# One hundred and twenty-eight products on a buffer of zeros, in sixteen groups, behind the clock-keeping products of an attention and gated-MLP kernel

## The chip, the cores and the metric

The kernel runs on one core of one Trainium2 chip. The metric is the device time of one execution in microseconds, as the median of several runs. The host only lays the arrays out.

## The reference

Attention inside chunks of 64 positions (8 batches, 8 heads, 576 positions, 64 channels), followed by an MLP with a spatial gate (model width 512, inner width 1024):

```python
# q, k, v: (8, 8, 576, 64), cut into 9 chunks of 64 positions
scores = matmul(q_c, k_c.T) / 8
attn = softmax(scores)                       # inside a chunk
x = matmul(attn, v_c)                        # laid out as (8, 576, 512)
h = gelu_tanh(x @ w_in)                      # (8, 576, 1024)
u, v = h[..., :512], h[..., 512:]
v_n = (v - mean(v)) / sqrt(var(v) + 1e-6) * g_ln
v_s = einsum('ts,bsd->btd', w_sg, v_n) + b_sg
out = x + (u * v_s) @ w_out
```

All inputs are float32. The three weight matrices reach the chip as 64-bit words and `w_sg` as float32.

## The kernel before

**The work.** The 8 batches of 576 positions make 36 attention tiles of 128 rows (two chunks each). For each batch there are four or five `v` units (`v_unit`, 128 tokens by 512 columns), four `u` units, four `s` units and four `o` units. Nearly every large product is taken three times, on a high and a low part of each operand in `F32R`, so that float32 accuracy is kept: a `v` unit is 12 products of 512 columns (L452), a `u` unit 24 of 288 columns (L489), an `s` unit 28 of 288 (L509), an `o` unit 24 of 288 (L532).

**The order.** `START` is a table of steps written out by hand for the first two batches; behind it a loop goes through the units of the other six, with attention steps in slots between them. The tile framework then schedules what the steps record, engine by engine, so the order on an engine is not that of the table. Its first steps are

```python
L0 A0 L1 A1 L2 L3 A4 W0 S0 W1 D8 w0 S1 W2 T0 w1 S2 O0 T1 W3 w2 S3 O1 T2 M0 w3 S4 O2 T3 v00 ...
```

`L` loads a weight block and `A` an attention tile, both on the SP queue. `W` (`pair_begin`) splits a block of `w_in` on VectorE and ScalarE (L130 to L133, L162, L166, L174); `w` (`pair_end`) makes its low part on TensorE (L178: a float32 product, two bf16 products and an `F32R` product, all of 512 columns) and takes it out on ScalarE (L179), and then loads a further block over the staging tile. `S` is a tile's scores (L314, 16 products of 64 by 64) and softmax (L333 to L358), `T` its transposition (L366, L368), `O` its output (L398) and the split of that (`keep`, L94, L97, L428, L438). A softmax is done head by head on ScalarE for tiles 0, 2 and 4 (L344) and in whole on VectorE and ScalarE for the others (L346, L349).

**The place of the change.** `D8` calls `keep_clock(8)` (L573 to L577): eight float32 products of the 128 by 128 identity with itself into a PSUM tile that nobody reads. They stand behind the scores of tile 0 (`S0`) and ahead of `w0` on TensorE. `ident` is the float32 view of `ident_r`, which ScalarE casts to `F32R` (L103) from a tile that GpSimd fills (`make_identity`, in masks.py). In the staging, `wsg_106`, `wsg_111`, `wout_115` and `wout_117` are the tiles of the blocks of `W0` to `W3`; `low_86` and `low_87` are two scaled bf16 identities. The tile `v` of the first `v` unit is taken from pool `mp` under the tag `v`, of which there is one buffer.

Of the kernel before, what the change touches and what calls it, by code (L numbers as in the profile page):

```python
# [10 lines left out]
F32 = mybir.dt.float32  # L11
F32R = mybir.dt.float32r
# [3 lines left out]
BF16 = mybir.dt.bfloat16  # L16
# [6 lines left out]
P = 128  # L23
DM = 512
DF = 1024
DH = DF // 2
# [54 lines left out]
def block_attention_gated_mlp(ctx: ExitStack, tc: tile.TileContext, qkv, w_in, w_out, w_sg, g_ln, b_sg, out):  # L81
    nc = tc.nc
# [3 lines left out]
    mp = ctx.enter_context(tc.tile_pool(name="mp", bufs=1))  # L86
# [15 lines left out]
    ident_r = const.tile([P, P], F32R, name="ident")  # L102
# [470 lines left out]
    def keep_clock(n):  # L573

        spare = ps_m.tile([P, 2, 512], F32, name="pm")
        for _ in range(n):
            nc.tensor.matmul(spare[:, 0, :P], ident, ident, start=True, stop=True)  # L577

    steps["D"] = keep_clock
    steps["G"], steps["g"] = lambda k: load_w_sg(), split_w_sg  # L580
# [56 lines left out]
```

## Time and profile before

| what | value |
|---|---|
| timed runs | 507.87 and 510.36 us, median 509.12 us |
| profiled execution, first to last instruction (span) | 505.7 us |
| TensorE (PE) matmul busy | 493.4 us, 98% of the span, 5238 instructions |
| VectorE (DVE) busy | 339.2 us, 67% |
| ScalarE (ACT) busy | 274.2 us, 54% |
| GpSimd (POOL) busy | 70.0 us, 14% |
| share of the chain that ended last, by engine | PE 83%, DVE 7%, ACT 5%, DMA 3%, POOL 1% |
| read from HBM, written | 36.34 MB, 9.44 MB |

The page gives the profiled execution as its span alone; the median of the two timed runs is 3.4 us above that span. Rows give line, engine, operation, output and inputs with their shape, a count, and the busy time and mean duration of one. PE is a matmul, PEld the load of its stationary matrix; a float32 product is recorded as two matmuls, an `F32R` or bf16 product as one. Matmuls are pipelined, so that the duration of one (0.40 us for 512 columns in L452) is longer than the time from its start to the next one's start. What a product costs in a stream is therefore read from starts and counts, not from durations.

### The profile page before, as it was taken

Reading aid. Unit: us, or ns where it says so; the run is one execution under the profiler, and the core shown is the slowest. Engines: PE = TensorE matmul, PEld = TensorE weight load, DVE = VectorE, ACT = ScalarE, POOL = GpSimd, SP = SyncE. Lnnn points to the kernel's source line nnn. Section 1 sums busy time; section 2 is a strip of 40 time slices with the busy share of each in tenths; the row PEclk is TensorE's granted clock in tenths of the full one; section 3 lists DMA queues with packets and bytes.
Section 4 is the critical chain, followed back from the end, with each engine's and each line's share of the span. In section 5 each row is a group of like instructions: output and inputs, shape, how many; then the busy total and the mean of one; then the engine's idle time right before and its main releaser. Section 6 shows DMA issues by size and latency. Waiting matters only on the chain.

```text
span 505.7 us, 12377 instructions
## 1 busy us (share of the span) xinstructions
PE 493.4 (98%) x5238; PEld 457.1 (90%) x5244; DVE 339.2 (67%) x707; ACT 274.2 (54%) x509; POOL 70.0 (14%) x72
## 2 busy tenths in 40 slices
PE   5999999999999999999999999999999999999996
PEld 4667899799998899989999899989999899999996
DVE  7998779987856947585563966676565776536141
ACT  5898667843346674355552774355643766334210
POOL 0112100210201401022100311022100131002000
PEclk9999999999999999999999999999999999999999
DMA  8958010237166113341324204160415200010002
GB/s 336 331 144 224 3 43 2 85 97 197 48 201 199 55 36 93 101 119 46 82 73 148 64 1 128 47 174 2 126 37 160 87 1 3 23 73 0 1 1 93
DMA packets 49595, 46.58 MB, mean 92 GB/s; under 512 B 35202, under 2 KB 39554, under 8 KB 49540
## 3 DMA queue, kind: packets, MB, share of 16 engines
q1 hardware_dynamic: 49540, 45.80, 29.9%
q8 instruction: 41, 0.67, 0.6%
q14 instruction: 14, 0.11, 0.1%
HBM read 36.34 MB, written 9.44 MB: 91 GB/s over the span
## 4 chain that ended last, share of the span: by engine, by line
PE 83%; DVE 7%; ACT 5%; DMA 3%; POOL 1%; issue 1%; DVEq 0%; SPq 0%; ACTq 0%; POOLq 0%
PE pm L509 20%; PE pm L532 19%; PE pm L489 18%; PE pm L452 17%; PE banks L322 3%; PE pm L410 3%; DMA qkv_t<-qkv 2%; PE pm L178 2%; DMA st<-w_out 1%; ACT pt L344 1%; PE pm L314 1%; POOL sm L461 1%; DVE v L470 1%; DVE gl L97 1%; PE pm L577 1%
## 5 line engine op out<-in xcount | busy, mean ns | idle before, releaser
L509 PE MATMUL pm<-wsg,v 128*128 128x288 f32 x768 | 107.9, 296 | 0.0
L509 PEld LDWEIGHTS pm<-wsg,v 128*128 128x128 f32 x768 | 103.9, 189 | 0.3
L532 PE MATMUL pm<-gh,wout 128*128 128x288 f32 x512 | 92.3, 297 | 0.0
L532 PEld LDWEIGHTS pm<-gh,wout 128*128 128x128 f32 x512 | 76.1, 189 | 0.5
L461 POOL TENSOR_TENSOR sm<-sm,neg_half 128x1 f32<-128x1 f32 x36 | 36.6, 1017 | 164.9 <-DVE sm L460 161.5
L358 POOL TENSOR_TENSOR pt<-pt,den 128x512 f32<-128x512 f32 x27 | 29.7, 1113 | 202.2 <-DVE den L357 128.3
L94 ACT CAST gh<-gt 128x576 fp32r<-128x576 f32 x32 | 21.5, 673 | 63.5 <-DVE gt L513 63.5
L532 PE MATMUL pm<-gl,wout 128*128 128x288 f32 x256 | 55.4, 296 | 0.0
L489 PE MATMUL pm<-xh,win_l 128*128 128x288 f32 x256 | 55.4, 298 | 0.0
L489 PE MATMUL pm<-xh,win_h 128*128 128x288 f32 x256 | 55.0, 296 | 0.0
L489 PE MATMUL pm<-xl,win_h 128*128 128x288 f32 x256 | 55.0, 296 | 0.0
L452 PE MATMUL pm<-win_h,xl 128*128 128x512 f32 x128 | 51.6, 403 | 2.0 <-DVE sm L460 0.9
L452 PE MATMUL pm<-win_l,xh 128*128 128x512 f32 x128 | 50.8, 397 | 0.0
L452 PE MATMUL pm<-win_h,xh 128*128 128x512 f32 x128 | 50.7, 396 | 0.0
L513 DVE TENSOR_TENSOR gt<-pm,u 128x576 f32<-128x576 f32 x32 | 24.1, 754 | 39.2 <-PE pm L509 39.1
L540 DVE TENSOR_TENSOR ot<-pm,xf 128x576 f32<-128x576 f32 (+1 forms) x33 | 24.1, 732 | 29.9 <-PE pm L532 29.8
L489 PEld LDWEIGHTS pm<-xh,win_l 128*128 128x128 f32 x256 | 41.5, 188 | 1.0
L532 PEld LDWEIGHTS pm<-gl,wout 128*128 128x128 f32 x256 | 41.5, 189 | 0.0
L489 PEld LDWEIGHTS pm<-xh,win_h 128*128 128x128 f32 x256 | 41.0, 188 | 0.0
L489 PEld LDWEIGHTS pm<-xl,win_h 128*128 128x128 f32 x256 | 41.0, 189 | 0.0
L97 DVE TENSOR_TENSOR xl<-pm,xh 128x512 fp32r<-128x512 f32 (+1 forms) x34 | 21.8, 640 | 26.4 <-ACT xh L94 26.4
L458 DVE BATCH_NORM_STATS2 sm<-hs 128x6 f32<-128x512 f32 x36 | 24.8, 688 | 19.8 <-ACT hs L455 19.6
(121 smaller groups left out, 816.7 us busy)
## 6 DMA issues: line engine op xcount, KB each, us to landing
qkv_t<-qkv SPq DMA_DIRECT2D x32, 512.0 KB, 4.5
out_dram<-ot SPq DMA_DIRECT2D x31, 288.0 KB, 2.1
qkv_t<-qkv SPq DMA_DIRECT2D x124, 64.0 KB, 3.6
qkv_t<-qkv SPq DMA_DIRECT2D x3, 768.0 KB, 11.9
wsg<-w_in SPq DMA_DIRECT2D x4, 512.0 KB, 6.4
wout<-w_in SPq DMA_DIRECT2D x4, 512.0 KB, 6.0
st<-w_out SPq DMA_DIRECT2D x8, 256.0 KB, 3.1
stage<-w_sg SPq DMA_DIRECT2D x5, 288.0 KB, 3.7
```

The source lines that it names most:

```text
L94: nc.scalar.copy(hi, src)
L97: lo_eng.tensor_tensor(lo, src, hi.bitcast(F32), op=ALU.subtract)
L322: nc.tensor.matmul(sc[o, c, h // 2, :], qt[r, 0, h, :], qt[r, 1, h, :], start=True, stop=True)
L358: (nc.gpsimd if t > last[1] else pick(f"n{t}")).tensor_tensor(pt, pt, den.unsqueeze(2).broadcast_to([P, H, D]), op=ALU.mult)
L452: nc.tensor.matmul(pv, a[:, kt, tok], c[:, kt, DH:], start=(i == 0), stop=(i == 11))
L458: nc.vector.bn_stats(st, h)
L461: nc.gpsimd.tensor_tensor(rs, rs, neg_half, op=ALU.pow)
L489: nc.tensor.matmul(pm[:, j, :HS], a[:, kt, dc], c[:, kt, j * HS : (j + 1) * HS], start=(i == 0), stop=(i == 11))
L509: nc.tensor.matmul(pm[:, j, :HS], a[:, dc], c[:, m, j * HS : (j + 1) * HS], start=(i == 0), stop=(i == len(ops) - 1))
L513: nc.vector.tensor_tensor(gt.rearrange("p (a c) -> p a c", a=2), pm[:, :, :HS], u2[0][:, dt, :].rearrange("p (a c) -> p a c", a=2), op=ALU ...
L532: nc.tensor.matmul(pm[:, j, :HS], a[:, kt, ec], c[:, kt, j * HS : (j + 1) * HS], start=(i == 0), stop=(i == len(ops) - 1),)
L540: nc.vector.tensor_tensor(ot[:, js], pm[:, js, :HS], res[:, js], op=ALU.add)
```

## The change

`keep_clock` also takes a tile `scr` of 4096 `F32R` columns from the pool and tag of `v`, has GpSimd write zeros to its first 2048 columns, and, behind the eight products, takes sixteen groups of eight products into the same unread PSUM tile. The stationary matrix is `ident_r` in twelve groups and a piece of the zeros, seen as bf16, in four. The moving matrix is always a piece of the zeros:

| groups | type | columns | pattern |
|---|---|---|---|
| 1 to 8 | `F32R` | 512, 512 (from column 2 on), 384, 288, 256, 192, 128, 64 | contiguous |
| 9 | `F32R` | 512 | every second element |
| 10, 11 | `F32R` | 2 x 256 | contiguous; with a gap of 256 between the halves |
| 12 | `F32R` | 256 x 2 | the same two elements 256 times |
| 13 to 15 | bf16 | 512, 288, 128 | contiguous |
| 16 | bf16 | 512 | every second element |

The diff, whole:

```diff
     def keep_clock(n):
 
         spare = ps_m.tile([P, 2, 512], F32, name="pm")
+        scr = mp.tile([P, 8, DH], F32R, name="scr", tag="v").rearrange("p a c -> p (a c)")
+        nc.gpsimd.memset(scr[:, :2048].bitcast(F32), 0.0)
+        half = scr.bitcast(BF16)
         for _ in range(n):
             nc.tensor.matmul(spare[:, 0, :P], ident, ident, start=True, stop=True)
+        w = ident_r
+
+        def group(a, c, k=8, m=P):
+            shape = c.shape[1:]
+            o = spare[:m, 0, : math.prod(shape)]
+            if len(shape) == 2:
+                o = o.rearrange("p (a b) -> p a b", a=shape[0])
+            for _ in range(k):
+                nc.tensor.matmul(o, a, c, start=True, stop=True)
+
+        group(w, scr[:, :512])
+        group(w, scr[:, 2:514])
+        group(w, scr[:, :384])
+        group(w, scr[:, :288])
+        group(w, scr[:, :256])
+        group(w, scr[:, :192])
+        group(w, scr[:, :128])
+        group(w, scr[:, :64])
+        group(w, scr[:, :1024].rearrange("p (a b) -> p a b", b=2)[:, :, 0].unsqueeze(1).broadcast_to([P, 1, 512]))
+        group(w, scr[:, :512].rearrange("p (a b) -> p a b", a=2))
+        group(w, scr[:, :1024].rearrange("p (a b) -> p a b", a=2)[:, :, :256])
+        group(w, scr[:, :2].unsqueeze(1).broadcast_to([P, 256, 2]))
+        group(half[:, :P], half[:, :512])
+        group(half[:, :P], half[:, :288])
+        group(half[:, :P], half[:, :128])
+        group(half[:, :P], half[:, :1024].rearrange("p (a b) -> p a b", b=2)[:, :, 0])
```

The scheduler puts the groups where they were written on TensorE, between the eight products and `w0`. This is the head of the difference on TensorE (the line of the eight products moves from L577 to L580; the bf16 groups have their weight loads in rows of their own):

```order
-L577 MATMUL pm<-ident 128x128 x8
+L580 MATMUL pm<-ident 128x128 x8
+L589 MATMUL pm<-scr,ident 128x512 x16
+L589 MATMUL pm<-scr,ident 128x384 x8
+L589 MATMUL pm<-scr,ident 128x288 x8
+L589 MATMUL pm<-scr,ident 128x256 x8
+L589 MATMUL pm<-scr,ident 128x192 x8
+L589 MATMUL pm<-scr,ident 128x128 x8
+L589 MATMUL pm<-scr,ident 128x64 x8
+L589 MATMUL pm<-scr,ident 128x512 x32
+L589 LDWEIGHTS scr
+L589 MATMUL pm<-scr 128x512
```

Nothing of the program's own work on TensorE stands between the eight products and the last group; the first product of `w0` follows the last group.

On ScalarE the scheduler moves the cast that makes `ident` (L103), near the start of the program:

```order
 L174 ACTIVATE win_h<-wsg_106 128x512
+L130 ACTIVATE wsg_111<-wsg_111 128x512
+L344 ACTIVATE pt,den<-pm,nmax 128x64 x2
 L103 CAST ident<-eye 128x128
 L108 ACTIVATE low_86<-eye 128x128
 L108 ACTIVATE low_87<-eye 128x128
-L130 ACTIVATE wsg_111<-wsg_111 128x512
+L344 ACTIVATE pt,den<-pm,nmax 128x64 x6
```

The cast stood ahead of the softmax of tile 0 (L344) and now stands behind its first two heads.

On VectorE the preparation of blocks 2 and 3 (`wout_115`, `wout_117`) moves ahead of the softmax of tile 1 (L333, L346):

```order
 L358 TENSOR_TENSOR pt<-pt,den 128x512
-L333 TENSOR_REDUCE nmax<-pm 128x8
 L131 TENSOR_SCALAR wout_115<-wout_115 128x512
-L346 TENSOR_TENSOR pt<-pm,nmax 128x512
 L132 TENSOR_SCALAR wout_115<-wout_115 128x512
 L131 TENSOR_SCALAR wout_117<-wout_117 128x512
 L133 SCALAR_TENSOR_TENSOR wout_115<-wout_115 128x512
-L355 TENSOR_REDUCE den<-pt 128x8
+L132 TENSOR_SCALAR wout_117<-wout_117 128x512
 L162 TENSOR_SCALAR wout_115<-wout_115 128x512
-L356 TENSOR_SCALAR den<-den 128x8
-L132 TENSOR_SCALAR wout_117<-wout_117 128x512
```

All ten operations on the two blocks now stand ahead of the first one that needs the scores of tile 1. ScalarE's four on them (L130 and L174, twice) move likewise, ahead of the first L179. On GpSimd the new memset stands between the memset and the select that make the identity. Behind the start, from the `u` units of the first batch on, TensorE's order is unchanged.

## The prediction, made before the run

> **What bounds the kernel now.** I read the head of the page first, then the windows, then the chain in order of time.
>
> ```profile
> span 505.7 us, 12377 instructions
> PE 493.4 (98%) x5238; PEld 457.1 (90%) x5244; DVE 339.2 (67%) x707; ACT 274.2 (54%) x509; POOL 70.0 (14%) x72
> ```
>
> ```profile
> core 0: us, PE busy (x) PEld busy (x) DVE busy (x) ACT busy (x) POOL busy (x), PEclk, DMA share, GB/s
> 10.50:20.00 9.50, 9.50 (x137) 6.24 (x140) 9.09 (x21) 7.82 (x22) 1.28 (x1) 1.00 1.02 391
> 20.00:30.00 10.00, 9.28 (x135) 6.77 (x131) 9.39 (x20) 9.32 (x42) 1.27 (x1) 1.00 0.76 224
> 30.00:40.00 10.00, 9.03 (x66) 5.98 (x66) 9.21 (x22) 9.77 (x19) 1.98 (x2) 1.00 0.55 156
> 40.00:60.00 20.00, 20.00 (x179) 15.71 (x184) 16.43 (x34) 15.85 (x31) 4.67 (x4) 1.00 0.44 113
> 60.00:100.00 40.00, 39.09 (x442) 35.70 (x432) 35.65 (x84) 29.61 (x55) 2.40 (x3) 1.00 0.14 41
> 100.00:500.00 400.00, 399.80 (x4248) 380.42 (x4247) 251.02 (x512) 196.81 (x332) 57.70 (x56) 1.00 0.27 78
> ```
>
> TensorE is the bound of the whole run. From 10.5 to 500 us it is idle for 0.72 + 0.97 + 0.91 + 0.20 = 2.8 us. Only between 20 and 40 us are VectorE and ScalarE as full as it is.
>
> ```profile
> 5.75 1.97 PE pm L314 x32
> 7.72 2.78 PE pm L577 x16
> 10.50 1.53 PE pm L178 x4
> ...
> 17.33 0.59 ACT xf L428
> ...
> 20.85 2.38 ACT pt L344 x16
> ...
> 37.76 1.43 PE pm L452 x5
> ...
> 44.17 5.60 PE pm L452 x24
> 49.77 3.20 PE pm L489 x24
> ```
>
> The chain is TensorE's up to 17.3 us, with the clock-keeping products (L577) on it. It then goes over ScalarE, GpSimd and VectorE to 37.76 us, and stays on TensorE from there. New work at 10.3 us is thus on the chain, and what stands behind it can give back no more than TensorE's 2.8 us of idle time.
>
> **The groups.** What a product costs in a stream is the time from start to start. The chain gives it for `F32R`: 5.60/24 = 0.233 us for 512 columns (L452), 3.20/24 = 0.133 us for 288 (L489), both about 0.456 ns a column. The next rows give bf16 and float32.
>
> ```profile
> 13.54 1.02 PE L178 MATMUL pm<-wsg,ident 128*128 128x512 f32 x2
> 14.40 0.60 PE L178 MATMUL pm<-wsg,low 128*128 128x512 bf16 x2
> ...
> 22.95 0.38 PE L178 MATMUL pm<-wout,low 128*128 128x512 bf16 x1
> ```
>
> Two bf16 products of 512 columns end 0.60 - 0.38 = 0.22 us later than one, so a bf16 product costs 0.216 to 0.22 us, 0.42 ns a column. A float32 product takes two recorded passes of (14.40 - 13.54)/2 = 0.43 us, 1.68 ns a column in all.
>
> - Six `F32R` groups of 512 columns (1, 2, 9 to 12): 48 x 0.233 = 11.2 us. The row shows contiguous columns only. For the patterns I take the same price. The bound above is 0.43 us, the one-pass price of the float32 row, because a pattern can halve the rate at which columns come in; below, 0.216 us, as bf16.
> - 384, 288 and 256 columns: 8 x (0.175 + 0.133 + 0.117) = 3.4 us by the same price a column.
> - 192, 128 and 64 columns: no `F32R` product of fewer than 288 columns runs before. Below, by columns, they cost 8 x (0.087 + 0.058 + 0.029) = 1.4 us. Above, at the float32 price, 8 x (0.32 + 0.223 + 0.117) = 5.3 us; 0.223 is L577's price (below) and 0.117 is two passes with a few ns each on top. I take the upper end, because L577, on the same identity with 128 columns of 4 bytes, is the nearest row.
> - bf16: 16 x 0.216 = 3.5 us for the two groups of 512 (the strided one at the contiguous price; above, 0.43), 8 x 0.122 = 1.0 us for 288 and 8 x 0.054 = 0.4 us for 128.
>
> The sum is 24.8 us; with 0.3 us for changes between forms, **25.1 us**, or 0.196 us a product. Products that are not dependent run without a wait: the zeros come from GpSimd long before.
>
> ```profile
> L245 POOL MEMSET wsg<- 64x576 f32 x1 | 0.6, 576 | 4.9 <-PE pm L452 4.9
> masks.py:197 POOL MEMSET eye<- 128x128 f32 x1 | 0.2, 204 | 0.3 <-POOLq L626 0.3
> ```
>
> The slope is (576 - 204)/(576 - 128) = 0.83 ns a column, so 2048 columns take about 1.8 us. They delay the identity by that much, near the start, while its first use (L103, below) is at 7.32 us. The tile `v` is not needed before the first `v` unit, behind the groups.
>
> The Trainium skill ("TensorE: Matmul & The Clock Gate", "Back-to-back issue gap") gives about 131 ns per product of 512 columns and 81 ns per product of 128 in a stream of loads and products. By that the groups would cost about half; this trace has 233 and 216 ns for 512 columns, and the measurement decides.
>
> **The cast that moved.** The eight products need `ident`.
>
> ```profile
> 7.32 0.28 ACT L103 CAST ident<-eye 128x128 fp32r<-128x128 f32 x1
> ...
> 9.24 0.31 ACT L344 ACTIVATE pt<-pm,nmax 128x64 f32<-128x64 f32 x1 [0.68 <-DVE nmax L340]
> 9.45 0.19 ACT L344 ACTIVATION_READ_ACCUMULATOR pt<-pm,nmax 128x1 f32 x1
> 9.54 0.30 ACT L344 ACTIVATE pt<-pm,nmax 128x64 f32<-128x64 f32 x1
> 9.74 0.20 ACT L344 ACTIVATION_READ_ACCUMULATOR pt<-pm,nmax 128x1 f32 x1
> 9.83 0.31 ACT L344 ACTIVATE pt<-pm,nmax 128x64 f32<-128x64 f32 x1
> ```
>
> Now the cast stands behind two heads, whose first can't start before VectorE's maximum is there at 9.24. It runs where the third head ran, at 9.83, and ends at 10.11. So the eight products begin at about 10.15 instead of 7.65, and TensorE is idle for 2.4 us behind the scores of tile 0. That takes away the filling which the products were. Their own cost depends on the clock:
>
> ```profile
> 8.24 0.85 PE L577 MATMUL pm<-ident 128*128 128x128 f32 x3
> ...
> 8.88 1.62 PE L577 MATMUL pm<-ident 128*128 128x128 f32 x11
> ...
> 9.67 0.83 PE L577 MATMUL pm<-ident 128*128 128x128 f32 x6
> ...
> 10.11 0.39 PE L577 MATMUL pm<-ident 128*128 128x128 f32 x2
> 10.34 0.59 PE L178 MATMUL pm<-wsg,ident 128*128 128x512 f32 x1
> ```
>
> Up to about 9.3 us a pass costs (8.88 - 8.24)/3 = 0.213 us, afterwards (10.11 - 9.67)/4 = 0.11 us: the clock doubles 3.6 us after the first product at 5.75. All fast, the 16 passes take 1.95 us with a first gap of 0.16 and end at 12.1; all slow, 3.6 us and 13.7. Before, they ended at 10.34. The delay is 1.8 to 3.4 us; I take **2.7 us**, since the idle stretch may or may not put the release off.
>
> The Trainium skill (same page, "What's actually happening") has the full clock granted after one busy window of about 3.4 us and taken away after one that is idle, with free-running windows. Windows that end at 9.34 and 12.75 would be an estimate from that figure; by it the passes end at about 13.2 and the delay is 2.9 us, within the bounds.
>
> **What waits behind the groups, and what that gives back.** On TensorE `w0`, `S1` and all later work are queued behind them. On VectorE the softmax of tile 1 waits for `S1`, on ScalarE the first L179 waits for `w0`, and on SP the `u` loads (L206) wait to overwrite the staging of `w0`. So nearly everything shifts with TensorE. The ten operations of VectorE on blocks 2 and 3 and the four of ScalarE are done under the groups instead, and the loads on their way, at a DMA share of 1.02 up to 20 us, land under them. That thins two full engines, but only TensorE's idle time can be won back, 0 to 2.8 us. ScalarE, which is at 9.3 and 9.8 of 10 us there, keeps the long run of heads (L344) on the chain. I take **1.5 us** back.
>
> **The sum.** 505.7 + 25.1 + 2.7 - 1.5 = 532.0 us of span. The median of the runs shown lies 3.4 us above the span of the profiled execution; with that the time is **535.4 us**, 5% more. The bounds: low 1.8 + 21.2 - 2.8 = 20.2 us more, 529.3; high, without anything given back and the largest delay, 28.5 us, 537.6, and beyond that only with the patterns.
>
> **Rivals.**
>
> *Short `F32R` products cost by their columns.* Then the three short groups take 1.4 instead of 5.3 us, and the time is 531.5. For it: from 512 to 288 columns the price goes exactly with the columns. Against: nothing shorter is shown, and L577 is four times dearer. Chance 0.25.
>
> *The patterns read at half rate.* If groups 2 and 9 to 12, or some of them, cost 0.43 us instead of 0.233, each adds 8 x 0.197 = 1.6 us; all five 7.9 us, 543.3; bf16 with a stride adds 1.7. For it: `F32R` already falls short of bf16's rate by 8%, as though operands of 4 bytes came in slowly. Against: the float32 rate is that of more passes and may have nothing to do with reading. Chance that it adds 5 us or more: 0.20, at 541 to 546.
>
> *Products of a group overlap in the array.* The 64 by 64 products do:
>
> ```profile
> 11.96 1.15 PE L314 MATMUL pm<-qkv_t 64*64 64x64 f32 x32
> ```
>
> 32 in 1.15 us is 0.036 us each. If two full-size products ran at once, the groups would cost 12.6 us and the time would be 523. Nothing in L452 or L577 shows it, though L577's products do not add to each other either. Chance 0.03; the skill's 131 ns would be this case.
>
> *The groups cost next to nothing (the other side).* At the price of the 64 by 64 products, 128 x 0.036 = 4.6 us, the time is 509.1 + 4.6 + 2.7 - 1.5 = 515, not slower by 2%. The place is TensorE between `S0` and `w0`; it decides if a product costs under (10.2 + 1.5 - 2.7)/128 = 0.07 us. The same side is reached if the products, whose results nobody reads, don't come to run at all: 509 to 512 us. Against both: L577's 16 passes are recorded at full price, and nobody reads them. Chance 0.03.
>
> **How the numbers follow.** The forecast has 0.49, the others 0.25, 0.20, 0.03 and 0.03. The likeliest time is 535.4. The range reaches from the low bound to the case of the patterns, 529 to 544; outside are the two cheap cases and the dearest patterns. Slower by over 2% (10.2 us, about what a measurement of this kernel can tell from no change): 0.97, from all cases but the last. Within 2%: 0.02; faster: 0.01.
>
> **What would show it.** Right: L589 as the new piece on the chain, 128 products in about 25 us between the eight products and L178; `F32R` at 0.233, 0.175, 0.133 and 0.117 us from 512 to 256 columns, and a jump up between 256 and 192; the cast at about 9.8 us and TensorE idle from 7.7 to 10.1; the stretch from L178 to the end 0 to 3 us shorter than before. Wrong: short products under 0.1 us, a strided or repeated group near 0.43 us, TensorE at the eight products before 9 us, or new idle time of TensorE behind the groups.

## The result and the profile after

The time went from 509.12 us (two runs, 507.87 and 510.36) to 536.0 us (535.89 and 536.12). The ratio on record is 1.055 with a 95% interval of [1.052, 1.059]; that is the ratio to the faster run of before (507.87), while to the median of the two it is 1.053. The profiled execution has a span of 534.3 us instead of 505.7, 28.6 us more. In two of the kernels further down one execution took over twice as long as the others (1312.82 and 1230.83 us); it is left out of their times.

The head of the page after:

```profile
span 534.3 us, 12645 instructions
PE 518.7 (97%) x5372; PEld 476.8 (89%) x5372; DVE 339.2 (63%) x707; ACT 274.7 (51%) x509; POOL 71.0 (13%) x73
```

TensorE's busy time grew by 25.3 us, while VectorE's did not change and ScalarE's hardly did (0.5 us). The rest of the 28.6 us is idle time of TensorE. The chain in order of time shows where the first part of that lies:

```profile
9.30 0.70 ACT pt L344 x4
10.00 0.20 ACT ident L103
...
10.24 3.78 PE pm L580 x16
14.02 24.80 PE pm L589 x128
38.83 1.53 PE pm L178 x5
...
46.20 2.37 ACT pt L344 x16
...
66.72 0.96 PE pm L452 x3
```

Before, the chain went from the scores of tile 0 straight to the eight products. Now it leaves TensorE for the maximum of tile 0, two heads and the cast (L103), and comes back at 10.24. TensorE's timeline has the idle time there (in brackets, with what ended it):

```profile
10.24 3.78 PE L580 MATMUL pm<-ident 128*128 128x128 f32 x16 [2.46 <-ACT ident L103]
```

The groups (L589) are the new piece. Behind them the chain goes over ScalarE and VectorE, as before, and returns to TensorE at 66.72. It leaves TensorE again later, from 99.61 to 120.8 us for the longest time, and so did the chain of before, from 70.67 us on. The prediction's reading that the chain stays on TensorE from 37.76 us on goes too far, then; its sum does not use it, since it goes by TensorE's idle time.

The windows view, restricted to L589 and cut at the first product of each group, gives the price of each. The columns are the stretch, its length, the busy time of PE and of PEld with the number of instructions in progress (some of a neighbouring group among them), the granted clock, the DMA share and GB/s. The length over eight is the time from one product's start to the next one's:

```profile
13.68:16.55 2.88, 2.88 (x8) 2.31 (x9) 1.00 1.02 425
16.55:18.42 1.87, 1.87 (x9) 1.51 (x8) 1.00 0.58 226
...
20.87:21.80 0.93, 0.93 (x10) 0.93 (x9) 1.00 0.00 0
21.80:22.67 0.87, 0.87 (x10) 0.87 (x9) 1.00 0.00 0
...
23.54:24.40 0.86, 0.86 (x10) 0.86 (x10) 1.00 0.00 0
24.40:28.19 3.79, 3.79 (x10) 1.74 (x10) 1.00 0.00 0
...
31.94:33.69 1.75, 1.75 (x9) 1.33 (x8) 1.00 0.00 0
33.69:35.43 1.74, 1.74 (x9) 0.80 (x9) 1.00 0.00 0
...
36.86:38.67 1.81, 1.81 (x11) 0.67 (x8) 1.00 0.00 0
sum 24.99, PE 24.99 PEld 18.60; mean PE 1.56 PEld 1.16
```

Read down the second column. 512 contiguous columns cost 1.87/8 = 0.233 us, as in L452. Group 1, the same product, costs 1.0 us more: its second to fifth products start 0.427 us apart and its last ones 0.233. The granted clock of 1.00 in its row does not speak against a slow clock, as the view counts a stretch without a clock record as 1.00. In the trace of the change the records begin at 15.72 us, with the full clock, and that is where the price falls. In the trace of before they begin at 9.34, where the price of a pass of the eight products fell from 0.213 to 0.11 us. In this document "the release" is the start of these records. From 512 to 256 columns (0.117) the price falls with the columns. From 192 to 64 it hardly falls any more: 0.11 us a product, and PEld is busy all the time there. Group 9, every second element, costs 0.474, twice the contiguous price. The offset, the halves and the gap (groups 2, 10 and 11) cost what a contiguous row does, the same two elements 256 times over 0.218, less than that. The two bf16 rows at the end are 0.217 contiguous and 0.226 for every second element.

The windows behind the groups, all engines:

```profile
48.00:58.00 10.00, 9.19 (x145) 6.85 (x141) 8.90 (x20) 9.36 (x34) 2.74 (x2) 1.00 0.89 254
58.00:68.10 10.10, 8.18 (x64) 5.40 (x63) 9.86 (x23) 9.22 (x17) 1.98 (x2) 1.00 0.44 136
...
88.20:128.30 40.10, 39.35 (x478) 36.08 (x479) 35.12 (x83) 30.11 (x56) 1.88 (x3) 1.00 0.14 41
```

TensorE is idle for 0.81 + 1.92 + 0.75 = 3.5 us there and 0.1 in the 400 us behind, against 2.8 before. From the first L178 to the end are 534.3 - 38.67 = 495.6 us, against 505.7 - 10.34 = 495.4. So nothing came back. The two larger of its four waits up to 68.1 us, from the timeline of TensorE (the other two are 0.36 and 0.46 us; one of 0.75 us follows at 120.8):

```profile
59.86 0.50 PE L452 MATMUL pm<-win_h,xl 128*128 128x512 f32 x1 [1.29 <-DVE xl L97]
...
66.70 0.50 PE L452 MATMUL pm<-win_h,xl 128*128 128x512 f32 x1 [0.63 <-DVE sm L460]
```

**What remained to be tested.** My theory after the result: the 28.6 us are the stream of the groups (25.0 us), each at a price of its own, and the late cast (3.3 us); nothing comes back since the idle time behind is a chain of latencies and not a lack of free time on VectorE and ScalarE. The rivals: that the cast's delay is hidden or worth less; that the new prices belong to the zeros, to the place or to the clock and not to type, columns and pattern; and that the idle time would have come back if the freed engines had been used better.

### The profile page after: what moved, and what is told of

It reads as the page before. It is cut to its first block, busy times and chain, and to the rows that moved or that the text cites. A ratio compares the mean times of both kernels' runs of the same rounds, so it can differ in the third digit from the quotient of the medians.

```text
span 534.3 us, 12645 instructions
## 1 busy us (share of the span) xinstructions
PE 518.7 (97%) x5372; PEld 476.8 (89%) x5372; DVE 339.2 (63%) x707; ACT 274.7 (51%) x509; POOL 71.0 (13%) x73
## 4 chain that ended last, share of the span: by engine, by line
PE 88%; DVE 7%; ACT 2%; DMA 1%; issue 1%; POOL 0%; DVEq 0%; SPq 0%; ACTq 0%
PE pm L509 20%; PE pm L489 19%; PE pm L532 18%; PE pm L452 17%; PE pm L589 5%; PE banks L322 3%; PE pm L410 3%; PE pm L178 1%; DMA qkv_t<-qkv 1%; PE pm L314 1%; PE pm L580 1%; ACT pt L344 1%; DVE gl L97 1%; DVE gt L513 1%; DVE blocks L372 0%
## 5 line engine op out<-in xcount | busy, mean ns | idle before, releaser
L461 POOL TENSOR_TENSOR sm<-sm,neg_half 128x1 f32<-128x1 f32 x36 | 35.6, 990 | 165.0 <-DVE sm L460 161.7
L452 PE MATMUL pm<-win_h,xl 128*128 128x512 f32 x128 | 51.6, 403 | 2.7 <-DVE sm L460 1.4
L452 PE MATMUL pm<-win_l,xh 128*128 128x512 f32 x128 | 50.7, 396 | 0.0
L452 PE MATMUL pm<-win_h,xh 128*128 128x512 f32 x128 | 50.6, 396 | 0.0
L513 DVE TENSOR_TENSOR gt<-pm,u 128x576 f32<-128x576 f32 x32 | 24.1, 753 | 39.3 <-PE pm L509 39.3
L540 DVE TENSOR_TENSOR ot<-pm,xf 128x576 f32<-128x576 f32 (+1 forms) x33 | 24.1, 732 | 29.9 <-PE pm L532 29.9
L97 DVE TENSOR_TENSOR xl<-pm,xh 128x512 fp32r<-128x512 f32 (+1 forms) x34 | 21.8, 640 | 26.2 <-ACT xh L94 26.2
```

The source lines that it names most:

```text
L97: lo_eng.tensor_tensor(lo, src, hi.bitcast(F32), op=ALU.subtract)
L452: nc.tensor.matmul(pv, a[:, kt, tok], c[:, kt, DH:], start=(i == 0), stop=(i == 11))
L461: nc.gpsimd.tensor_tensor(rs, rs, neg_half, op=ALU.pow)
L513: nc.vector.tensor_tensor(gt.rearrange("p (a c) -> p a c", a=2), pm[:, :, :HS], u2[0][:, dt, :].rearrange("p (a c) -> p a c", a=2), op=ALU ...
L540: nc.vector.tensor_tensor(ot[:, js], pm[:, js, :HS], res[:, js], op=ALU.add)
```

## The experiments

### The cast and the groups, each by itself

One kernel is the change with a copy of one column on GpSimd ahead of the memset; nothing reads the column, but the scheduler then puts the cast ahead of the softmax again.

```diff
         scr = mp.tile([P, 8, DH], F32R, name="scr", tag="v").rearrange("p a c -> p (a c)")
+        nc.gpsimd.tensor_copy(scr[:, :1], eye[:, :1])
         nc.gpsimd.memset(scr[:, :2048].bitcast(F32), 0.0)
```

> The same sixteen groups; GpSimd's memset now stands behind the select that makes the identity (a one-column copy of it into the zeros' tile ahead of the memset ties them), so the cast of ident stands again ahead of the softmax of tile 0. Theory (the late cast costs its idle time on TensorE and a slow clock that reaches into the groups): the eight products start at about 7.65 us instead of 10.24, the clock is up at about 9.4, the groups take 24.0 us instead of 25.0, and the first product behind them starts at about 34.4 instead of 38.7: 4 us less than the changed kernel, about 532. Rival (TensorE was waiting for something else there as well, or what is won in front is lost behind): under 1.5 us less.

It took 532.52 us against 507.56 on the same chip, ratio 1.048 [1.046, 1.050], 3.5 us less than the change, about as expected.

```profile
7.53 2.61 PE L581 MATMUL pm<-ident 128*128 128x128 f32 x16
9.90 19.29 PE L590 MATMUL pm<-scr,ident 128*128 128x512 f32 x96
...
34.00 1.02 PE L178 MATMUL pm<-wsg,ident 128*128 128x512 f32 x2
```

The rows are the eight products, the first groups and the first L178. There is no idle time ahead of the eight products. The groups take 34.00 - 9.90 = 24.1 us, 0.9 less than in the change, because the full clock is there before they begin (release at 8.73 us). The first L178 comes 4.67 us earlier, and the span is 529.6, 4.7 us shorter. So in these two executions the late cast costs 3.3 us ahead of the groups and 0.9 in the first group; the remaining 0.4 us is the earlier release here than in the kernel before (8.73 against 9.34). The profiled execution is also the fastest of the four (531.40 us against 532.46 to 532.58), so that 4.7 us is too much and 3.5, from the medians, the better figure.

The other keeps the tile, the memset and the late cast and leaves the groups out:

```diff
-        group(w, scr[:, :512])
...
-        group(half[:, :P], half[:, :1024].rearrange("p (a b) -> p a b", b=2)[:, :, 0])
```

> The groups are left out, the tile of zeros, its memset and the moved cast stay. Theory: the eight products start at about 10.2 us as in the changed kernel, mostly at the slow clock, and the first product behind them at about 13.7 instead of 10.3: 2 to 3.5 us more than before, about 512, and 25 us less than the changed kernel. Rival (the late cast is hidden by what VectorE and ScalarE do meanwhile): the time of before within 1 us.

It took 513.70 us against 507.56, ratio 1.011 [1.009, 1.013]. That is 6.1 us for the late cast and the order that comes with it, more than the delay at the start. The first two rows are of this kernel, the last is of the kernel before:

```profile
10.07 3.79 PE L580 MATMUL pm<-ident 128*128 128x128 f32 x16 [2.46 <-ACT ident L103]
...
36.83 0.50 PE L452 MATMUL pm<-win_h,xl 128*128 128x512 f32 x1 [2.66 <-DVE xl L97]
```

```profile
31.36 0.50 PE L452 MATMUL pm<-win_h,xl 128*128 128x512 f32 x1 [0.87 <-DVE xl L97]
```

The first L178 is at 13.65, 3.3 us later than before, and 2.9 us more are lost behind it. Half of that is idle time of TensorE (8.0 us from the first L178 to the end instead of 6.6), above all in the wait shown (2.66 instead of 0.87 us). The other half is busy time (490.2 us instead of 488.8): behind that wait the granted clock is 0.50 from 38.30 to 41.71 us. VectorE's order is not that of the change. Only four of its ten operations on blocks 2 and 3 stand ahead of tile 1's softmax, and VectorE then waits 1.75 us for tile 1's scores. Its maximum of tile 4 comes 5.0 us later than before (32.40 us instead of 27.43), 1.7 more than the delay of the start. What sets this 1.7 is not shown; no run isolates it. The late cast is thus worth 6.1 us without the groups and 3.5 with them (medians), and the groups 536.0 - 513.7 = 22.3 us on top of it. The two parts of the change do not add.

One more thing bears on the slow clock. Five executions have the cast this late and TensorE idle for 2.46 us ahead of the eight products, which start at 10.04 to 10.24 us; their releases lie at 13.13, 13.21, 13.88, 14.41 and 15.72 us. Five others have no idle time there and the eight products at 7.47 to 7.65; their releases lie at 8.73, 9.02, 9.34, 10.93 and 11.93. The row below is of the last one, the kernel before with one pin (further down). It has no idle time, and yet 3.78 us of slow passes, as many as the change:

```profile
7.56 3.78 PE L579 MATMUL pm<-ident 128*128 128x128 f32 x16
```

So the late cast does put the release off, but by how much is different in each execution, by up to 3.2 us. The change's own release, 15.72, is the latest of its five, and the 1.0 us in its first group is partly chance.

### Short products

The groups of the change are replaced by other short ones, on fewer columns and on fewer stationary columns, for their prices alone (one execution).

```diff
...
+        group(w, zer[:, :240])
+        group(w, zer[:, :224])
+        group(w, zer[:, :32])
+        group(w[:, :64], zer[:, :192], m=64)
+        group(w[:, :64], zer[:, :128], m=64)
+        group(w[:, :64], zer[:, :64], m=64)
+        group(w[:, :32], zer[:, :64], m=32)
+        group(ident, zer[:, :64].bitcast(F32))
+        group(half[:, :P], half[:, :64])
...
```

> Other groups of eight in the same place, to price short products; only the prices are read. Theory (loading the 128 stationary columns of 4 bytes sets the floor of 0.111 us): F32R with 240, 224 and 32 moving columns 0.111 us each; with 64 stationary columns 0.087, 0.058 and 0.056 us for 192, 128 and 64 moving columns; with 32 stationary ones 0.03 us; float32 with 64 columns 0.22 us, two loads. Rival (a fixed floor for each product with 4-byte operands, whatever is loaded): 0.111 us with 64 and 32 stationary columns too. Second rival (the columns count, as the prediction's upper end had it): float32 with 64 columns 0.117 us. For bf16 the load theory, by bytes, gives 0.056 us for 64 and 32 moving columns on 128 stationary ones and 0.028 on 64; without it 0.027 and 0.014.

Windows cut at the starts of the groups: 32 columns, then 64 columns on 64 and on 32 stationary columns, then 64 columns in bf16 on 128:

```profile
15.27:16.09 0.82, 0.82 (x10) 0.82 (x9) 1.00 1.06 435
...
17.32:17.75 0.44, 0.44 (x11) 0.44 (x10) 1.00 0.62 211
17.75:18.02 0.26, 0.26 (x11) 0.26 (x10) 1.00 0.21 78
...
19.83:20.06 0.23, 0.23 (x10) 0.23 (x10) 1.00 0.00 0
```

With 128 stationary columns 240 (0.112), 224 (0.111) and even 32 moving columns cost about 0.11 us. With 64 stationary columns the floor is 0.44/8 = 0.055 (0.058 in the steady steps), with 32 it is 0.033. The floor goes with the stationary columns, 0.9 to 1.0 ns a column of 4 bytes, and not with the output, as bf16 products with 128 output rows and 64 moving columns go far below it: it is the loading of the weights. With 64 stationary columns 192 moving ones cost 0.088 us, by their columns again. A float32 product of 64 columns takes two passes of 0.112, so my float32 row was that same floor paid twice. The Trainium skill ("TensorE: Matmul & The Clock Gate", "LDWEIGHTS (loading the stationary operand)") has the load take P/1.2 ns for P columns; by it I estimate 107, 53 and 27 ns for 128, 64 and 32. The 0.112, 0.058 and 0.033 us here lie 5 to 6 ns above that. In bf16 the load is no such floor here: eight products with 128 stationary and 64 moving columns took 0.23 us, 0.029 each, a quarter of 0.112, and with 32 moving columns 0.025 each.

### Strides

> Other groups of eight in the same place, 512 columns each, to price patterns of the moving operand; only the prices are read (the first group partly at the slow clock). Theory (the moving operand is read at about 8.7 bytes of address per ns, wanted or skipped): F32R with steps 2, 3, 4 and 8: 0.47, 0.70, 0.94 and 1.9 us; two of four and four of eight: 0.47 us; bf16 with steps 2, 3, 4, 8: 0.23, 0.35, 0.47, 0.94; two of four 0.23. Rival (any step other than one halves the rate of F32R once, as single elements come in instead of pairs): 0.47 us for steps 2, 3, 4 and 8, 0.233 for two of four and four of eight; bf16 0.226 for every step.

```diff
...
+        full = lambda a, s, n=512: a[:, : n * s].rearrange("p (a b) -> p a b", b=s)[:, :, 0]
+        flat = lambda a: a.unsqueeze(1).broadcast_to([P, 1, a.shape[1]])
         group(w, scr[:, :512])
+        group(w, flat(full(scr, 2)))
...
+        group(w, flat(full(scr, 8)))
+        group(w, scr[:, :1024].rearrange("p (a b) -> p a b", b=4)[:, :, :2])
+        group(w, scr[:, :1024].rearrange("p (a b) -> p a b", b=8)[:, :, :4])
         group(half[:, :P], half[:, :512])
+        group(half[:, :P], full(half, 2))
...
+        group(half[:, :P], full(half, 8))
...
```

One execution. Windows: first `F32R` in steps of 2, two of every four and four of every eight (the 0.46 of its last step is the change to bf16), then bf16 in steps of 2, 4 and 8. The last step of each bf16 row already carries the next pattern, so that the steady steps are a little less than an eighth of it:

```profile
18.36:21.96 3.60, 3.60 (x9) 1.64 (x8) 1.00 0.01 3
...
32.71:36.34 3.62, 3.62 (x9) 1.66 (x8) 1.00 0.00 0
36.34:38.47 2.13, 2.06 (x9) 1.46 (x9) 1.00 0.00 0
...
40.20:42.12 1.91, 1.91 (x9) 0.76 (x8) 1.00 0.00 0
...
44.93:49.00 4.06, 4.06 (x9) 0.93 (x8) 1.00 0.00 0
49.00:55.70 6.70, 6.70 (x9) 0.97 (x8) 0.72 0.00 0
```

The two types follow two rules, and neither theory holds for both. `F32R` costs 0.43 to 0.46 us for any step from 2 to 8 and for runs of two (8 bytes), and 0.233 again for runs of four (16 bytes). Of the patterns with gaps, those that break up 16 bytes about halve the rate once and no further; the pair of the change that is repeated without gaps is none of them. For bf16 the steady steps are 0.226, 0.340, 0.451 and 0.900 us, in proportion to the bytes passed over, with the step of 2 still nearly free. The Trainium skill ("SBUF — State Buffer", "Specifications (TRN2)") has lines of 16 bytes that need two hits each for the full rate. By that a step of 2 on 4-byte elements, with two hits a line, would be free; here it costs twice as much, and the measurement decides. A step of 2 on bf16 has four hits a line and is nearly free (0.226 against 0.216).

The last row has a granted clock of 0.72 although TensorE is busy throughout; the clock record there falls to 0.50 at 51.91 us. That led to the next run.

### Does a slow reader count as busy?

```diff
...
+        group(w, scr[:, 512:1024])
+        group(w, scr[:, 3072:3584])
+        group(w, flat(full(scr, 8)), k=24)
+        group(half[:, :P], half[:, :512])
+        group(half[:, :P], half[:, :1024].rearrange("p (a b) -> p a b", b=4)[:, :, :2])
+        group(half[:, :P], full(half, 8), k=16)
         group(half[:, :P], half[:, :512])
```

> Groups in the same place, to price once more and to watch the clock; only prices and the clock are read. F32R with 512 contiguous columns at three places of the zeros, then 24 F32R products with step 8, then bf16: 8 contiguous, 8 with two of four, 16 with step 8, 8 contiguous. Theory (the clock is granted by how many columns come through in a stretch of time, so products that wait for their operand count as idle): it stays up in the F32R products with step 8 (0.43 us each) and falls to one half during the bf16 products with step 8 (0.90 us each), so that the contiguous ones behind them cost 0.43 us. Rival (TensorE always has work, so the clock stays up; the drop seen once was chance): 0.216 us for them. Bf16 two of four: 0.226 us if address counts, 0.45 if runs do. The three places of the zeros: 0.233 us each, or one at 0.227 if the place matters.

One execution. Windows: the last eight of 24 `F32R` products in steps of 8, then the second eight of 16 bf16 products in steps of 8, and contiguous bf16 behind them:

```profile
28.84:32.53 3.69, 3.62 (x9) 1.57 (x9) 1.00 0.00 0
...
43.93:50.63 6.70, 6.70 (x9) 1.02 (x8) 0.50 0.00 0
50.63:53.62 2.99, 2.99 (x8) 0.91 (x6) 0.50 0.00 0
```

`F32R` at 0.431 us a product keeps the full clock for ten microseconds. bf16 at 0.900 us a product loses it, 4.7 us after the first of them (36.73 to 41.39): the mean is 0.82 over the first eight, 0.50 over the next, and the contiguous products behind cost 2.99/7 = 0.427 instead of 0.216 (the trace has seven of the eight). These are the prices that the theory gave. Whether it is columns that are counted, as it has it, or something else that a product of 0.900 us lacks, they do not tell. A PE row that is full is thus no proof that the clock holds. Bf16 in runs of two of every four costs 0.226 us, as in steps of 2, so for bf16 the address range counts and not the runs. Contiguous `F32R` groups on three places of the buffer cost 0.2335 us a product (the first one once its slow start is over), so the place does not matter.

### The same products late in the run and on data

48 contiguous `F32R` products and 8 with every second element, on `win_h` instead of zeros, stand behind the last `u` unit of batch 4 of the kernel before.

```diff
...
+        for k in range(48):
+            nc.tensor.matmul(o, ident_r, win_h[:, k % KT, :512], start=True, stop=True)
+        for k in range(8):
+            c = win_h[:, k % KT, :].rearrange("p (a b) -> p a b", b=2)[:, :, 0]
+            nc.tensor.matmul(o, ident_r, c.unsqueeze(1).broadcast_to([P, 1, 512]), start=True, stop=True)
...
```

> The kernel before with 48 F32R products of 512 contiguous columns and 8 of every second column, on ident and the high words of w_in instead of zeros, behind the last u unit of batch 4; the output is not used, and nothing is moved at the start. Theory (each product costs TensorE its price and nothing is hidden or given back where TensorE has no idle time): 48 x 0.233 + 8 x 0.47 = 15.0 us more than before, the prices as on zeros. Rival (zeros are cheaper than data): a higher price per product. Rival (the other engines' work that piles up is made up for, so part comes back): under 13 us more.

It took 522.68 us against 507.42, ratio 1.030 [1.028, 1.031], or 15.3 us more, as expected.

```profile
301.95 11.07 PE L584 MATMUL pm<-win_h,ident 128*128 128x512 f32 x48
312.86 3.78 PE L587 MATMUL pm<-win_h,ident 128*128 128x512 f32 x8
...
316.57 1.16 PE L410 MATMUL pm<-ptT,qkv_t 64*64 64x64 f32 x64
```

The stream takes (312.86 - 301.95)/48 = 0.227 us for contiguous and 3.71/8 = 0.464 for every second element, 14.6 us together. The median is 15.3 us longer, the span of the profiled execution, the fastest of the four, 14.0. The prices belong to type and pattern within 3%, not to the zeros or the start, and in a stretch where TensorE never waits all of it goes into the time.

### Why nothing came back: the preparation

In two kernels the `u` blocks' preparation (L130 on) is held in the order in which it was written, so that it can't be pulled ahead; in the change, and in the kernel before.

```diff
-        nc.scalar.activation(f.bitcast(F32), hw.bitcast(F32), AF.Abs, scale=2.0**16)
+        first = nc.scalar.activation(f.bitcast(F32), hw.bitcast(F32), AF.Abs, scale=2.0**16)
+        if pinned:
+            tc.keep_in_program_order(first)
...
```

> The changed kernel, with the preparation of the u blocks (X steps) pinned on ScalarE behind what the program has recorded there before it, so that it no longer stands ahead of the softmaxes and splits that TensorE waits for behind the groups. Theory (what the groups took off VectorE and ScalarE was filled by the scheduler with this preparation, which then stands in the chain): TensorE's waits of 0.36, 0.46, 1.29 and 0.63 us behind the groups shrink to under 1.2 us together, its idle time from the first product behind the groups to the end falls from 3.6 to about 2 us, and the time by 1 to 2 us. Rival (the chain of softmax, split and first v units is as long by its own steps, whatever stands between): idle time and time within 0.5 us of the changed kernel.

> The kernel before with the same pin and nothing else. If the preparation in the chain costs anything before the change, it is at most TensorE's 1.6 us of idle time between 10 and 40 us: 0 to 1.5 us less than before. If the preparation is then late for the u units, TensorE waits there and the time is longer by up to 2 us.

The change with it took 541.63 us, ratio 1.068 [1.066, 1.070] to the kernel before, some 5.6 us more than the change; the kernel before with it took 514.53, ratio 1.013 [1.012, 1.015]. VectorE in the first of them:

```profile
56.97 0.17 DVE L358 TENSOR_SCALAR den<-den 128x8 f32<-128x8 f32 x1 [2.92 <-ACT pt L346]
...
58.02 0.68 DVE L97 TENSOR_TENSOR xl<-banks,xh 128x512 fp32r<-128x512 f32 x1
```

VectorE now stands still for 2.92 us, so it has time to spare, and TensorE nevertheless waits 1.59 us for the low part of x (L97) at 58.76. My explanation that the freed time had only been filled with other preparation fell with this. VectorE waits for ScalarE's eight heads of tile 4 (L344 of the change, two lines further down here), 2.49 us one behind the other, and TensorE waits for what comes behind them. ScalarE had itself stood idle for 1.48 us ahead of these heads. Later TensorE waits 1.65 us for a copy on ScalarE (`xf`, L432 of the change) and 1.11 and 0.79 us for the `u` units' blocks, whose preparation was held back. Behind these waits the clock is lost for a while in both kernels, 0.50 from 91.64 to 95.05 us in the first and from 66.54 to 69.96 in the second, so that the 5.6 and 7.1 us are not waiting alone.

### Why nothing came back: the heads of tile 4

```diff
-ACT_SOFTMAX = (0, 2, 4)
+ACT_SOFTMAX = (0, 2)
```

This takes the softmax of tile 4 in whole, with VectorE's part, instead of head by head on ScalarE. First in the change:

> The changed kernel with the softmax of tile 4 in whole on VectorE and ScalarE (one exponential of 0.6 us and two more VectorE passes of 0.7 us) instead of head by head on ScalarE (2.4 us). Theory (behind the groups TensorE waits for a chain of steps, in which the eight heads of tile 4 stand ahead of the split of tile 2, and not for engines that are full): its wait for xl of 1.3 us goes, and with it 1 to 2 us of the time. Rival (VectorE's throughput is the limit there): the two more passes on VectorE make the waits as long or longer, and the time is the same or up to 1 us more.

It took 533.59 us against 508.05, ratio 1.050 [1.048, 1.051], 2.4 us less than the change. Up to 100 us only two waits of TensorE of over 0.2 us are left behind the groups, both quoted here:

```profile
52.01 0.66 PE L366 MATMUL banks<-ident,pt 128*128 128x128 f32 x4 [0.36 <-ACT xf L428]
...
53.50 1.15 PE L398 MATMUL banks<-ptT,qkv_t 64*64 64x64 f32 x32 [0.46 <-ACT ptT L368]
```

The waits of 1.29 and 0.63 us are gone. From the first L178 (37.73) to the end (530.9) are 493.2 us, 2.4 less than in the change; that the first L178 itself comes 0.9 us earlier is mostly the earlier release (13.88 instead of 15.72). So 2 us and more could be won back under the groups; what stood in the way was the chain of heads. VectorE's throughput is excluded, since VectorE has two passes more here. The kernel also takes work off ScalarE; that ScalarE was not simply full rests on the change with the pin, where it stands idle ahead of the heads and TensorE waits all the same. The question was then whether the kernel before gains as well:

> The kernel before, with the softmax of tile 4 taken in whole on VectorE and ScalarE instead of head by head on ScalarE (ACT_SOFTMAX is (0, 2) instead of (0, 2, 4)); no groups, no change to the clock-keeping products. Theory (the chain through tile 4's eight heads sets TensorE's idle time behind the start, as it did with the groups): the stretch from the first L178 to the end is 1.5 to 2.5 us shorter than 495.4, the span about 503.5, the time about 507, 2 us less than the kernel before. Rival (without the groups VectorE is still full with the preparation of blocks 2 and 3 when tile 4 comes, so that the work moved to it is late): the idle time stays at 2.8 us or grows, and the time is the same or up to 2 us more.

It does not: 510.46 us against 507.63, ratio 1.006 [1.004, 1.007]. The rival was right on the side, with 2.8 us more, but not in the mechanism that it named. TensorE's largest wait, and ScalarE ahead of it:

```profile
60.60 1.16 PE L178 MATMUL pm<-wout,ident 128*128 128x512 f32 x2 [3.06 <-ACT u L496]
```

```profile
57.26 1.46 ACT L474 ACTIVATE z<-hs,sm 64x512 fp32r<-64x512 f32 x2 [2.53 <-POOL sm L461]
58.74 1.26 ACT L475 CAST z<-z 64x512 fp32r<-64x512 f32 x2
59.91 0.64 ACT L496 ACTIVATE u<-pm 128x576 f32<-128x576 f32 x1
```

Of the wait of 0.87 us for tile 4 only 0.21 are left, as the theory had it. But the scheduler, with another start, now puts the first `u` unit's eviction (L496) behind ScalarE's work on `z`, which waits 2.53 us for GpSimd (L461). TensorE has no PSUM tile free and stands for 3.06 us. Before, that eviction stood ahead of `z`, at 53.50 us. The first L178 is 0.7 us later too, because the eight products take 3.57 us instead of 2.78 at the slow clock; nothing waits ahead of them, so this is the later release of this execution (10.93 instead of 9.34).

Behind its release this execution was granted a clock of 0.95, not 1.00. Its float32 passes of 512 columns start 0.448 us apart instead of 0.430 and its bf16 products 0.224 instead of 0.216, but its `F32R` products cost what they did, 0.233 us for 512 columns and 0.133 for 288. So the price of `F32R` is not set by the clock there, and the executions at 1.00 take no less time (509.89 to 511.09 us against its 510.39).

### Products ahead of the scores

Ten bf16 products on zeros ahead of the scores of tile 0 might have the full clock granted earlier. In the first kernel VectorE writes the zeros behind its other memsets, in the second as its first operation of all (with the softmax of tile 4 in whole).

```diff
-L0 A0 L1 A1 L2 L3 A4 W0 S0 W1 D8 w0 S1 W2 ...
+L0 A0 L1 A1 L2 L3 A4 H10 W0 S0 W1 D8 w0 S1 W2 ...
...
+            nc.tensor.matmul(spare[:, 0, :], half[:, :P], half[:, :512], start=True, stop=True)
```

> The kernel before with ten bf16 products of 512 columns on zeros ahead of the scores of tile 0, where TensorE waits for the first load (zeros by VectorE). Theory (products cost nothing where TensorE is idle, and they bring the clock up earlier): the scores of tile 0 take 1.15 instead of 1.97 us and the eight products 1.9 instead of 2.7, so the first product behind them starts about 0.8 us earlier, 9.5 instead of 10.3, and the time is 0.5 to 1 us less than before, unless the order that the scheduler then makes costs more. Rival (the ten products reach past the arrival of the first tile, or the start is bound by VectorE): the same time within 0.5 us or up to 1 us more.

> The kernel before, with the softmax of tile 4 in whole, as in the run beside it, and ten bf16 products of 512 columns on zeros ahead of the scores of tile 0, as in the earlier run with products at the head, but the zeros (128 columns, read four times over) are VectorE's first operation of all instead of its sixth. Theory (there the zeros were late, at 4.88 us; the products themselves fit ahead of the first load): the products start at about 1.1 us, cost 0.427 us each at the slow clock, end by 5.4 us, ahead of the scores at 5.75, the clock is granted before the scores, which take about 1.15 us instead of 1.97, and the first L178 comes 0 to 0.9 us before 10.34: 0.5 us less than the run beside it, if the preparation of the first block does not set it. Rival (the first L178 waits for the split of the first block on VectorE and ScalarE, which is 0.1 us later for the memset): no difference, or up to 0.5 us more.

The first took 510.93 us against 508.05, ratio 1.005 [1.004, 1.006]. The zeros were there at 4.88 us only, the ten products ran at the slow clock until 9.26, and the scores stood behind them. That is 2.9 us more, beyond the rival's 1 us too. The second took 511.0 against 507.63, ratio 1.007 [1.005, 1.008]:

```profile
5.84 1.15 PE L316 MATMUL pm<-qkv_t 64*64 64x64 f32 x32 [0.42 <-DMA qkv_t<-qkv]
9.19 3.43 PE L579 MATMUL pm<-ident 128*128 128x128 f32 x16 [2.20 <-ACT ident L103]
```

The products at the head run from 0.98 to 5.4 us and do what they were meant to: the scores take 1.15 instead of 1.97 us. But the cast is late again, 2.20 us of waiting, the clock is lost over that (the eight products cost (12.45 - 9.19)/16 = 0.204 us a pass), and the first L178 comes 2.1 us later than before. Here the clock of the eight products stands in the records, a mean of 0.55:

```profile
9.19:12.45 3.26, 3.26 (x16) 3.26 (x17) 3.12 (x8) 3.26 (x20) 0.00 (x0) 0.55 1.04 420
```

Neither theory had this: it is the late cast of the change, from another cause. The cast stands on ScalarE behind the first operation on the second weight block (8.28 us), which waits 3.08 us for its load. From the first L178 to the end are 507.8 - 12.45 = 495.4 us, as in the kernel before. The long wait of 3.06 us is not in this trace, and still tile 4's softmax in whole gives nothing back without the groups. No version tried here is faster than the kernel before.

## Why the prediction was right, step by step

The predicted 535.4 us and the measured 536.0 lie close together. The mechanism was right, a longer stream on the engine that bounds the run, but that the number is so close is luck: the span was predicted 2.3 us too short, and the distance from span to median 1.7 us too long. Inside the groups the terms were off by 2.8 us one way and 2.7 the other.

| term | predicted, us | measured, us |
|---|---|---|
| six `F32R` groups of 512 columns | 11.2 | 14.0 |
| 384, 288 and 256 columns | 3.4 | 3.4 |
| 192, 128 and 64 columns | 5.3 | 2.6 |
| bf16 | 4.9 | 5.0 |
| changes between forms | 0.3 | in the rows |
| all groups | 25.1 | 25.0 |
| the late cast | 2.7 | 3.3 |
| given back (below 0) or lost behind the groups | -1.5 | 0.3 |
| sum on the span | 26.3 | 28.6 |
| median above the span | 3.4 | 1.7 |

- **What bounds the kernel**: held. TensorE's stream is lengthened by all that is put in; late in the run and on data, 14.6 us of products made 15.3 us of time by the medians and 14.0 by the spans.
- **`F32R` by columns down to 256, bf16 at 0.216, 0.122 and 0.054**: held within 0.01 us a product.
- **Short `F32R` products at the float32 price**: wrong in its size. L577 was the nearest row by type and columns, but its price is that of two passes; the price of one pass, 0.11 us, stood in the same row (16 passes). The 0.11 us is the floor set by loading 128 columns of weights. The jump up between 256 and 192 columns that I named as a sign did not come. The rival "by their columns" is wrong too, and the truth lies between the two bounds.
- **Patterns at the contiguous price**: right for the offset, the halves and the gap, wrong for every second element, which adds 1.9 us as the rival priced it (1.6 for a group), and slightly wrong for the repeated pair, which is cheaper by 0.1. The rival's five groups were too many; it came true for one. The other 1.0 us by which the 512-column groups missed is the slow clock in group 1, which belongs to the next point.
- **The cast**: the place held (9.90 against 9.83, TensorE idle for 2.46 us). All 16 passes ran at the slow clock, the end of the range that I had as 3.4. The step that failed is that the slow clock would end there: it went on into the first group for another 1.0 us, with the release at 15.72. The estimate of 12.75 counted on from the release of another execution, 9.34, as though its place were the same in each; with the cast as late it lay anywhere from 13.13 to 15.72 in five executions.
- **1.5 us given back**: wrong. What VectorE and ScalarE had done early thinned them only in the first 9.3 us behind the groups (busy for 5.6 and 5.5 us, before 9.0 and 7.9). In the 20.1 us behind that they are as full as before (18.8 and 18.6 us, before 18.7 and 18.9). But TensorE's idle time did not come from full engines. It is the chain through tile 4's eight heads on ScalarE; with that chain shortened, 2.4 us did come back. Without the groups the late cast loses 2.9 us more behind the start, so the change's groups hid a loss that I had not seen; its cause is open.
- **3.4 us between median and span**: too much. It is 1.7 after, and 1.8 in the later runs. The higher of the two runs of before put 1.2 us into it; the remaining 0.4 is not explained.

Why the products of every second `F32R` element cost 0.474 us in the change and 0.453 in the run of strides, and why a repeated pair is cheaper than a contiguous row, stays open.

## What to carry to other kernels

Where one engine bounds the whole run, price what is put into its stream by steady start-to-start times of the same type, width and pattern, and look for a floor from the weight load: with 128 stationary `F32R` columns nothing from 240 moving columns down gets cheaper, while reading every second 4-byte element doubles the price. Look in the order of every engine for what else a small edit moves: one memset on GpSimd moved a cast on ScalarE by 2.6 us, and that cost 3.5 us of the time with the groups and 6.1 without them. Where the clock changes over the stretch that you compare, look at its records and at several executions before you put a microsecond down to the edit. Free time on a waiting engine gives nothing back by itself; first follow the chain to see whether it is full or only waiting in turn.

## What the runs showed that I had not expected

- Loading 128 stationary columns of 4 bytes sets a floor of 0.112 us a product, 64 of them 0.058 and 32 of them 0.033; 128 stationary columns of bf16 take no more than 0.029.
- `F32R` read with gaps in pieces of under 16 bytes costs 0.43 to 0.47 us for 512 columns whatever the step, in pieces of 16 bytes 0.233; bf16 goes by the bytes passed over, up to 0.900 us at a step of 8.
- A stream of bf16 products at 0.900 us each keeps TensorE busy in the records and still loses the clock, down to 0.50; `F32R` products at 0.431 us each keep it.
- With 2.46 us of idle time ahead of the eight products the full clock came at 13.1 to 15.7 us in five executions, without it at 8.7 to 11.9 in five others. The place differs by about 3 us from one execution to the next, and two of those without idle time ran their passes at 0.213 us too.
- At a granted clock of 0.95 float32 passes and bf16 products cost 4% more, `F32R` products the same.
